# An attention and mixture-of-experts kernel: first loads interleaved, first scores placed behind four rounded half blocks

## The chip, the cores and the metric

The kernel runs on one core of a Trainium2 chip. The metric is the time of one execution in device microseconds (us). The core has five engines with a queue each: TensorE (PE, with its weight loads PEld), VectorE (DVE), ScalarE (ACT), GpSimd (POOL) and SyncE (SP), which only issues DMA transfers. An engine works through its own queue in the order in which the program was written out for it; semaphores order the engines among each other.

## What is computed

```python
def reference(**kwargs):
    attn_out = _attn_ref(**attn_kwargs)              # 4 batches, 8 heads, 576 positions, head size 64
    x = attn_out.transpose(0, 2, 1, 3).reshape(B * S, H * D)     # 2304 tokens x 512
    x = _moe_ref(x=x, **moe_kwargs)                  # (sigmoid(x @ w_gate) * (x @ w_val)) @ w_out
    return _moe2_ref(x=x, **moe2_kwargs)             # 8 experts, two per token, relu, 512 -> 1024 -> 512
...
def _attn_ref(q, k, v, phi):
    a = softmax(phi, axis=2)                         # over the positions, 32 memory slots per head
    k_m = np.einsum('bhsm,bhsd->bhmd', a, k)
    v_m = np.einsum('bhsm,bhsd->bhmd', a, v)
    attn = softmax(q @ k_m.T / sqrt(64))             # 32 scores per position and head
    return attn @ v_m
```

(The softmax lines are shortened here.) Everything is float32 at the interface.

## The kernel before, in words

**Stages.** The program opens with attention for batch 0 and with the preparation of the three weight matrices of the first network, runs the first network batch by batch while the attention of the next batch goes along, routes the tokens, and ends with the eight experts. The change touches the opening alone, about the first 50 us, but it moves instructions up to about 150 us. From there on all five queues hold the same instructions in the same order in both kernels.

**Preparing the weights.** The 18 blocks of `wg`, `wv` and `wo` (six of each, 128x1024 values of 64 bits) arrive as 36 half blocks through four buffers (`ws2`, `WB = 4`; a tile is named `w64`). `rounded` turns one half block into a rounded float32 half: ACT converts the low words (L335), DVE builds the high words in two instructions (`pw` at L337, then L338), POOL adds the two (L339). Only when POOL is done is the buffer free for the load of the half block four places on, which SP issues (L324). When both halves are there, ACT squares the block for its scale (L369; L365 for `wo`), and `norm2` (L92 to L101) makes a power-of-two scale out of the sum: a small matmul `pmx` and a few short DVE instructions, the first of which (L97) waits for that matmul.

**Attention of batch 0.** `features` exponentiates `phi` (DVE L216, ACT L218, DVE L219 and L220). `memory` turns it over on PE (L178, L181), copies it out on ACT (L179, L182), sums keys and values over the positions (PE L191, 40 instructions for each of two groups of heads, ACT L193), and puts the result into `kbd` and `vb` (PE L199, ACT L203 and L205). `values_scale` squares `vb` (ACT L228) and gives the scale `sv0` through `norm2`. `attention` then computes the scores in three pieces (PE L269 and L266; DVE L273, L277, L281 to L283; ACT L278; POOL L284), and turns them over into `x` (PE L292, ACT L299, DVE L300).

**First network.** For each of six units `u`, `fold` multiplies the values into the weights of gate and value (DVE L237, POOL L240, PE L247, ACT L249, DVE L250: called a fold below), and `stage1` runs three pieces of 24 matmuls each (L430) with ACT and DVE behind each (L433 to L437). Batch 1 follows with six more folds. The six blocks of `wo` are split in two halves of float16 by ACT and DVE (L382, L383), and `stage2` (L448) uses them.

**What sets the order.** The code hands out work in turns: a turn of `weights` is about one half block, a turn of `attentions` one step of the attention. A scheduler then orders each engine's queue by priority, where `ahead_by` moves the attention forward; `behind(d, o)` forces an instruction `d` behind an instruction `o`. Before the change, the first three turns go to the attention (its loads are already out by then), five to the weights, and then one of each in turn until `sv0` is known. The first maximum over the scores (L273) is forced behind the latest `pw`/L338 pair that was written out before it (`self.shifted`).

Of the kernel before, what the change touches and what calls it, by code (L numbers as in the profile page):

```python
# [67 lines left out]
class Kern:  # L68
# [16 lines left out]
    def norm2(self, pool, m, tag, before=1, n=1, floor=0):  # L85


        nc = self.nc
        for _ in range(before):
            yield  # L90
        pt = self.pr.tile([P, 512], F32, tag="pr", name="pmx")[:, :n]
        d = nc.tensor.matmul(pt, self.onef, m, start=True, stop=True)  # L92
        if self.mark is not None:
            self.behind(d, self.mark)

        h, s, iv = (pool.tile([P, n], I32, tag=tag + c, name=tag + c) for c in "hsi")
        nc.vector.tensor_scalar(h, pt.bitcast(I32), 24, 23, op0=ALU.logical_shift_right, op1=ALU.logical_shift_left)  # L97
        if floor:
            nc.vector.tensor_scalar(h, h, floor << 23, None, op0=ALU.max)
        nc.vector.tensor_scalar(s, h, -1, 204 << 23, op0=ALU.mult, op1=ALU.add)  # L100
        nc.vector.tensor_scalar(iv, h, 50 << 23, None, op0=ALU.add)  # L101
        return s.bitcast(F32), iv.bitcast(F32)

    def consts(self):
# [5 lines left out]
        self.idf = cp.tile([P, P], F32, name="idf")  # L110
        nc.vector.tensor_scalar(self.idf, jp, 0.0, None, op0=ALU.is_equal)
        self.onef = cp.tile([P, P], F32, name="onef")
# [48 lines left out]
    def att_first_loads(self, b):  # L161
        for x in (("phi", 0), ("phi", 1), ("kv0", 0), ("kv1", 0)):
            self.att_load(b, *x)
        self.wload_next()
        for x in (("kv0", 1), ("kv1", 1), ("q", 0), ("q", 1)):
            self.att_load(b, *x)
        for _ in range(WB - 1):
            self.wload_next()

# [40 lines left out]
    def features(self, b):  # L210

        nc, a2, al = self.nc, self.a2, self.al
        for g in range(2):
            t = al[(b, "phi", g)]
            mx = a2.tile([P, 1], F32, tag="pmx", name="pmx")
            nc.vector.tensor_reduce(mx, t, axis=AX.X, op=ALU.max, negate=True)  # L216
            sm = a2.tile([P, 1], F32, tag="psm", name="psm")
            nc.scalar.activation(t, t, AF.Exp, bias=mx, accum_out=sm)  # L218
            nc.vector.tensor_scalar(sm, sm, 1e-9, None, op0=ALU.add)  # L219
            nc.vector.reciprocal(sm, sm)  # L220
            self.rsum[(b, g)] = sm
            yield
# [30 lines left out]
    def attention(self, b):  # L253
# [4 lines left out]
        def scores(u):  # L258
# [17 lines left out]
            ex = (a2 if u < 2 else self.a1).tile([P, n, M], F32, tag="ex" if u < 2 else "ex2", name="ex")  # L276
            nc.vector.tensor_tensor(ex, sc, mx.unsqueeze(2).to_broadcast([P, n, M]), op=ALU.subtract)  # L277
            nc.scalar.activation(ex, ex, AF.Exp, scale=0.125)  # L278
# [52 lines left out]
    def rounded(self, t, v):  # L331
# [4 lines left out]
        w = self.px.tile([P, DM], F32, tag="px", name="pw").bitcast(I32)  # L336
        nc.vector.tensor_scalar(w, hi, 3, 0x3FFFFFFF, op0=ALU.logical_shift_left, op1=ALU.bitwise_and)  # L337
        self.shifted = nc.vector.scalar_tensor_tensor(v, hi, -0x40000000, w, op0=ALU.bitwise_and, op1=ALU.bitwise_or)  # L338
# [571 lines left out]
    def build(self):  # L910
# [26 lines left out]
        self.whalves = [(k, u, h) for k, u in self.wjobs for h in range(2)]  # L937
        self.wts, self.mark, self.wanted = [], None, []
        self.att_first_loads(0)
# [48 lines left out]
        turns(atts, atts, atts)  # L988
        turns(*[weights] * FIRST)
        while not self.tokens_ready:  # L990
            turns(*[weights] * (4 if self.sv else 1), atts)
# [154 lines left out]
```

## Time and profile before

| | |
|---|---|
| median of three timed runs | 881.49 us (880.47 to 883.07) |
| the profiled execution | 876.4 us |
| its span, from first to last instruction | 873.9 us |
| PE busy / DVE / ACT / POOL, whole span | 798.6 / 465.5 / 443.9 / 225.4 us |
| mean granted TensorE clock | 0.962 |

The span is cut into 40 equal slices of about 21.8 us on the profile's page; a digit there is the busy share in tenths. A row of the timeline reads: start in us, length in us, engine, line of the code, operation, what it writes and reads, how many; in brackets, how long the engine stood idle before it, and what ended that. SPq is SP's queue issuing a transfer. The lines are those of the code before.

### The profile page before, as it was taken

To read this page: it belongs to the slowest core of one execution; us is meant where nothing else is said; L and a number is where in the kernel's file an instruction comes from. 1 tells how busy PE (TensorE), PEld (TensorE's weight loads), DVE (VectorE), ACT (ScalarE), POOL (GpSimd) and SP (SyncE) were. 2 spreads that over 40 slices of the span, in tenths; PEclk is the share of its full clock that TensorE was granted. 3 is DMA by queue.
4 is the path that set the end of the run, shared out by engine and by line. 5 is a ranking of instruction groups with operands and counts; after the bars stand their busy time and mean duration, and the time that the engine had idled before them with its cause. 6 is when DMAs were issued, how large, how long until landed. Compare 5 with 4: busy or idle time off the path is not lost.

```text
span 873.9 us, 16775 instructions
## 1 busy us (share of the span) xinstructions
PE 798.6 (91%) x6531; PEld 524.7 (60%) x6531; DVE 465.5 (53%) x1269; ACT 443.9 (51%) x859; POOL 225.4 (26%) x237
## 2 busy tenths in 40 slices
PE   5157889999999988999999999999999999999995
PEld 4145767657667755766566555665747566574752
DVE  3788798545638687873453146644635435350210
ACT  4658757415554565672243356644736545461320
POOL 1565441001202130204114442102223132222112
PEclk9559889999999999999999999999999999999998
DMA  9778658432121566547692989536766757452113
GB/s 309 258 247 293 222 148 281 137 73 79 26 80 26 176 212 218 170 169 186 200 319 61 177 166 266 144 110 143 193 159 99 174 139 201 78 127 37 23 17 43
DMA packets 125841, 135.15 MB, mean 155 GB/s; under 512 B 71744, under 2 KB 88256, under 8 KB 125248
## 3 DMA queue, kind: packets, MB, share of 16 engines
q1 hardware_dynamic: 115712, 113.30, 44.2%
q0 software_dynamic: 10048, 20.76, 13.1%
q8 instruction: 52, 0.85, 0.4%
q14 instruction: 29, 0.24, 0.1%
HBM read 87.97 MB, written 30.86 MB: 136 GB/s over the span
## 4 chain that ended last, share of the span: by engine, by line
PE 72%; DVE 10%; DMA 9%; ACT 5%; issue 2%; POOL 1%; SPq 1%; POOLq 0%; DVEq 0%; ACTq 0%
PE py L791 23%; PE ph L777 21%; PE px L448 12%; PE pg L430 11%; DMA f<-w 2%; PE pv L247 2%; PE pa L269 1%; DVE hl L383 1%; DVE pw L337 1%; ACT hl L382 1%; DVE w L338 1%; DMA st<-kv 1%; DVE pg L435 1%; DMA xt<-row 1%; DMA w<-wo 1%
## 5 line engine op out<-in xcount | busy, mean ns | idle before, releaser
L430 PE MATMUL pg<-x,wq 128*128 128x192 f16 x1728 | 167.1, 254 | 16.0 <-ACT wq L249 7.2
L430 PEld LDWEIGHTS <-wq 128*128 128x128 f16 x1728 | 149.8, 101 | 34.8 <-issue 11.4
L791 PEld LDWEIGHTS <-hT 128*128 128x128 f16 (+1 forms) x960 | 99.8, 105 | 104.7 <-DVE hT L783 0.8
L448 PE MATMUL px<-wo,gT 128*128 128x512 f16 x648 | 148.8, 380 | 1.9 <-DVE ones L490 1.5
L797 POOL DMA_INDIRECT out<-y,mts x40 | 64.6, 1615 | 208.2 <-ACT y L796 206.1
L791 PE MATMUL py<-w2a,hT 128*128 128x512 f16 (+1 forms) x480 | 105.2, 379 | 0.3 <-DVE hT L783 0.3
L791 PE MATMUL py<-w2b,hT 128*128 128x512 f16 (+1 forms) x480 | 104.9, 379 | 0.0
L448 PEld LDWEIGHTS <-gT 128*128 128x128 f16 x648 | 62.0, 98 | 69.9 <-issue 5.2
L777 PE MATMUL ph<-xe,w1a 128*128 128x312 f16 (+2 forms) x768 | 103.3, 296 | 0.0
L777 PE MATMUL ph<-xe,w1b 128*128 128x312 f16 (+2 forms) x768 | 103.0, 296 | 0.0
L783 DVE TENSOR_TENSOR hT<-r,hT 128x312 f16<-128x312 f32 (+2 forms) x128 | 57.4, 480 | 83.8 <-ACT hT L782 83.3
L796 ACT ACTIVATE y<-py,css 128x512 f32<-128x512 f32 (+1 forms) x40 | 27.5, 686 | 131.3 <-PE py L791 126.8
L777 PEld LDWEIGHTS <-w1b 128*128 128x128 f16 x768 | 75.2, 98 | 27.1
L777 PEld LDWEIGHTS <-w1a 128*128 128x128 f16 x768 | 75.0, 98 | 27.1
L781 ACT ACTIVATE r<-ph 128x312 f32<-128x312 f32 (+2 forms) x128 | 49.7, 428 | 74.1 <-PE ph L777 69.1
L598 POOL DMA_INDIRECT meta<-mt,vi x36 | 37.2, 1033 | 123.7 <-DVE vi L595 98.5
L762 POOL DMA_INDIRECT xg<-xs,mts x40 | 43.9, 1098 | 86.0 <-DMA xe<-xg 53.0
L433 ACT ACTIVATE sg<-pg,gs 128x384 f32<-128x384 f32 x72 | 41.7, 579 | 43.0 <-PE pg L430 42.7
L435 DVE SCALAR_TENSOR_TENSOR pg<-sg,pg 128x384 f32<-128x384 f32 x72 | 40.2, 558 | 35.9 <-PE pg L430 22.7
L794 DVE TENSOR_TENSOR css<-mts,iw 128x1 f32<-128x1 f32 (+1 forms) x40 | 6.4, 163 | 94.5 <-ACT y L796 90.3
L782 ACT CAST hT<-r 128x312 f16<-128x312 f32 (+2 forms) x128 | 53.2, 458 | 0.9
L436 ACT ACTIVATE gT<-pg 128x384 f16<-128x384 f32 x72 | 34.9, 484 | 33.6 <-DVE pg L435 31.6
(314 smaller groups left out, 947.0 us busy)
## 6 DMA issues: line engine op xcount, KB each, us to landing
wo<-w SPq DMA_DIRECT2D x48, 512.0 KB, 5.1
st<-kv SPq DMA_DIRECT2D x16, 512.0 KB, 5.8
f<-w SPq DMA_DIRECT2D x16, 512.0 KB, 5.5
wsp<-hl SPq DMA_DIRECT2D x16, 512.0 KB, 3.5
w<-wg SPq DMA_DIRECT2D x12, 512.0 KB, 5.0
w<-wv SPq DMA_DIRECT2D x12, 512.0 KB, 4.8
w<-wo SPq DMA_DIRECT2D x12, 512.0 KB, 4.8
out<-z SPq DMA_DIRECT2D x23, 256.0 KB, 3.0
```

The source lines that it names most:

```text
L430: nc.tensor.matmul(p[:, f, :], w[:, l, g, j, f * P : (f + 1) * P], x[:, r, g, ch * QC : (ch + 1) * QC], start=n == 0, stop=n == 5)
L433: nc.scalar.activation(sg, ps[0], AF.Tanh, scale=self.gate_scale(b, u))
L435: nc.vector.scalar_tensor_tensor(pv, sg, 1.0, pv, op0=ALU.add, op1=ALU.mult)
L448: nc.tensor.matmul(p, g[:, l, f % 2, t * P : (t + 1) * P], self.wob[f // 2][:, r, f % 2, :], start=f + i == 0, stop=f == FT - 1 and i == 2)
L598: d = nc.gpsimd.indirect_dma_start(out=self.meta, out_offset=bass.IndirectOffsetOnAxis(ap=vi[:, t, k : k + 1], axis=0), in_=mt[:, t, k, :] ...
L762: self.nc.gpsimd.indirect_dma_start(out=xg.rearrange("p a b -> p (a b)"), out_offset=None, in_=self.xs[:rows, :], in_offset=bass.IndirectO ...
L777: nc.tensor.matmul(p[:, : t1 - t0], w1[:, l, k, f * P : (f + 1) * P], xe[:, x, t0:t1], start=n == 0, stop=n == 3 * KT - 1)
L781: nc.scalar.activation(r, p[:, : t1 - t0], AF.Relu, scale=2.0 ** -19)
L782: nc.scalar.copy(self.hT[:, 0, f, t0:t1], r)
L783: nc.vector.tensor_sub(self.hT[:, 1, f, t0:t1], r, self.hT[:, 0, f, t0:t1])
L791: nc.tensor.matmul(py, self.hT[:, l, f, i * P : i * P + m], w2[:, w, f, :], start=n == 0, stop=n == 3 * F2T - 1)
L797: d = nc.gpsimd.indirect_dma_start(out=self.out, out_offset=bass.IndirectOffsetOnAxis(ap=mt[:m, 0:1], axis=0), in_=y[:m], in_offset=None, ...
```

## The change

The first loads come in another order: in place of all keys, values and queries around one half block of weights, with the other three half blocks at the end, the half blocks now stand between the keys and the queries. After the five turns of the weights, turns go to the attention alone until the first scores are written out, so that four half blocks (and no more) stand ahead of them; the roundings that are written out later, and the first DVE instruction of every later `norm2`, are forced behind the first subtraction of the scores (`self.less`). The first instruction on `phi` is forced behind the making of the unit matrix `idf` (`self.made`).

```diff
         h, s, iv = (pool.tile([P, n], I32, tag=tag + c, name=tag + c) for c in "hsi")
-        nc.vector.tensor_scalar(h, pt.bitcast(I32), 24, 23, op0=ALU.logical_shift_right, op1=ALU.logical_shift_left)
+        d = nc.vector.tensor_scalar(h, pt.bitcast(I32), 24, 23, op0=ALU.logical_shift_right, op1=ALU.logical_shift_left)
+        if self.less is not None:
+            self.behind(d, self.less)
...
-        nc.vector.tensor_scalar(self.idf, jp, 0.0, None, op0=ALU.is_equal)
+        self.made = nc.vector.tensor_scalar(self.idf, jp, 0.0, None, op0=ALU.is_equal)
...
     def att_first_loads(self, b):
-        for x in (("phi", 0), ("phi", 1), ("kv0", 0), ("kv1", 0)):
-            self.att_load(b, *x)
-        self.wload_next()
-        for x in (("kv0", 1), ("kv1", 1), ("q", 0), ("q", 1)):
-            self.att_load(b, *x)
-        for _ in range(WB - 1):
-            self.wload_next()
+        for x in (("phi", 0), ("phi", 1), ("kv0", 0), ("kv1", 0), "w", ("kv0", 1), ("kv1", 1), "w", "w", ("q", 0), "w", ("q", 1)):
+            if x == "w":
+                self.wload_next()
+            else:
+                self.att_load(b, *x)
...
-            nc.vector.tensor_reduce(mx, t, axis=AX.X, op=ALU.max, negate=True)
+            d = nc.vector.tensor_reduce(mx, t, axis=AX.X, op=ALU.max, negate=True)
+            if b == 0:
+                self.behind(d, self.made)
...
-            nc.vector.tensor_tensor(ex, sc, mx.unsqueeze(2).to_broadcast([P, n, M]), op=ALU.subtract)
+            d = nc.vector.tensor_tensor(ex, sc, mx.unsqueeze(2).to_broadcast([P, n, M]), op=ALU.subtract)
+            if self.less is None:
+                self.less = d
...
-        nc.vector.tensor_scalar(w, hi, 3, 0x3FFFFFFF, op0=ALU.logical_shift_left, op1=ALU.bitwise_and)
+        d = nc.vector.tensor_scalar(w, hi, 3, 0x3FFFFFFF, op0=ALU.logical_shift_left, op1=ALU.bitwise_and)
+        if self.less is not None:
+            self.behind(d, self.less)
...
         turns(atts, atts, atts)
         turns(*[weights] * FIRST)
+        while self.less is None:
+            turns(atts)
```

What follows from it in the queues is shown at three places. A tile's number in the names tells tiles of one name apart; line numbers after L216 differ by 2 to 6 between the two kernels.

ACT's queue at the opening, before: `w64_151` is the first half block, `a_185` and `a_263` the turned-over `phi` of the first and second group of heads.

```order
L179 COPY a_185<-pa_186 128x512
L182 COPY a_185<-pa_192 64x128
L335 ACTIVATE w64_151<-w64_151 128x512
L193 ACTIVATE km_248<-pa_227,psm_175 128x256
L203 COPY kbd_136<-pa_257 64x2x32 x2
L205 COPY vb0_81<-pa_257 64x128
L179 COPY a_263<-pa_264 128x512
L182 COPY a_263<-pa_270 64x128
L193 ACTIVATE km_294<-pa_273,psm_181 128x256
```

The same place on ACT in the change, where `w64_159` and `w64_161` are the second and third half block.

```order
L339 ACTIVATE w64_151<-w64_151 128x512
L179 COPY a_185<-pa_186 128x512
L182 COPY a_185<-pa_192 64x128
L193 ACTIVATE km_247<-pa_226,psm_175 128x256
L339 ACTIVATE w64_159<-w64_159 128x512
L203 COPY kbd_136<-pa_249 64x2x32 x2
L179 COPY a_255<-pa_256 128x512
L205 COPY vb0_81<-pa_249 64x128
L182 COPY a_255<-pa_262 64x128
L339 ACTIVATE w64_161<-w64_161 128x512
L375 ACTIVATE wo0_71,wum_210<-w0_95 128x1024
L193 ACTIVATE km_286<-pa_265,psm_181 128x256
```

Three low-word conversions and a square now stand among the steps of `memory`; the first of them stands ahead of the copy that the sums of the first group wait for.

DVE's queue up to the first maximum of the scores (`smx`), before; `sv0h` is the first instruction of the values' scale and `w0h` that of the first weight scale.

```order
L338 SCALAR_TENSOR_TENSOR w1_96<-w64_171,pw_220 128x512
L337 TENSOR_SCALAR pw_251<-w64_201 128x512
L338 SCALAR_TENSOR_TENSOR w2_97<-w64_201,pw_251 128x512
L337 TENSOR_SCALAR pw_311<-w64_208 128x512
L97 TENSOR_SCALAR sv0h_324<-pmx_322 128x1
L97 TENSOR_SCALAR w0h_298<-pmx_296 128x2
L99 TENSOR_SCALAR sv0h_324<-sv0h_324 128x1
L338 SCALAR_TENSOR_TENSOR w2_97<-w64_208,pw_311 128x512
L100 TENSOR_SCALAR sv0s_325<-sv0h_324 128x1
L101 TENSOR_SCALAR sv0i_326<-sv0h_324 128x1
L273 TENSOR_REDUCE smx_340<-pa_331 128x16
```

DVE at the same place in the change; `w64_167` is the fourth half block, `w64_201` the fifth.

```order
L341 TENSOR_SCALAR pw_213<-w64_161 128x512
L344 SCALAR_TENSOR_TENSOR w1_96<-w64_161,pw_213 128x512
L97 TENSOR_SCALAR sv0h_299<-pmx_297 128x1
L341 TENSOR_SCALAR pw_220<-w64_167 128x512
L101 TENSOR_SCALAR sv0h_299<-sv0h_299 128x1
L344 SCALAR_TENSOR_TENSOR w1_96<-w64_167,pw_220 128x512
L102 TENSOR_SCALAR sv0s_300<-sv0h_299 128x1
L103 TENSOR_SCALAR sv0i_301<-sv0h_299 128x1
L275 TENSOR_REDUCE smx_315<-pa_306 128x16
L279 TENSOR_TENSOR ex_317<-pa_306,smx_315 128x512
L97 TENSOR_SCALAR w0h_354<-pmx_352 128x2
L341 TENSOR_SCALAR pw_327<-w64_201 128x512
```

Six half blocks stood ahead of the first maximum, now four do; the values' scale, which waits for PE, now stands ahead of the fourth half block, and the first weight scale ahead of the fifth.

DVE between the fifth and the sixth fold of batch 0, before: the second subtraction of the fifth fold (`wq_1326`), and the last two half blocks (`wo6`) behind it.

```order
L250 TENSOR_TENSOR wq_1326<-pv_1328,wq_1326 128x512
L338 SCALAR_TENSOR_TENSOR wo6_77<-w64_1236,pw_1385 128x512
L337 TENSOR_SCALAR pw_1390<-w64_1243 128x512
L237 TENSOR_SCALAR ws_1501<-w5s_1027,sv0s_325 128x2
L338 SCALAR_TENSOR_TENSOR wo6_77<-w64_1243,pw_1390 128x512
L435 SCALAR_TENSOR_TENSOR pg_1351<-sg_1376,pg_1351 128x384
```

DVE in the same stretch in the change; `ws_1473` is the scale of the sixth fold, whose subtractions come later still.

```order
L344 SCALAR_TENSOR_TENSOR wo5_76<-w64_1272,pw_1405 128x512
L441 SCALAR_TENSOR_TENSOR pg_1418<-sg_1443,pg_1418 128x384
L341 TENSOR_SCALAR pw_1449<-w64_1355 128x512
L443 SCALAR_TENSOR_TENSOR gT_1416<-pg_1418,gT_1416 128x2x192
L344 SCALAR_TENSOR_TENSOR wo5_76<-w64_1355,pw_1449 128x512
L341 TENSOR_SCALAR pw_1455<-w64_1363 128x512
L239 TENSOR_SCALAR ws_1473<-w5s_1129,sv0s_300 128x2
L344 SCALAR_TENSOR_TENSOR wo6_77<-w64_1363,pw_1455 128x512
L400 TENSOR_SCALAR gs05_1528<-w5i_1130,sv0i_301 128x1
L341 TENSOR_SCALAR pw_1535<-w64_1401 128x512
```

Between the fifth and the sixth fold's subtractions stood two half blocks, and now there are seven. Counted along DVE's queue, 16 half blocks are rounded ahead of the first fold's subtraction before and 13 in the change; 21 and 17 ahead of the second, 26 and 22, 31 and 27, 34 and 29 ahead of the third to fifth, and all 36 ahead of the sixth in both. Of the six splits of `wo`, five stood ahead of the seventh fold's subtraction, and now two do.

## Rows read from the trace of the kernel before

**Rows 1.** The profile's page: span, PE's total, and PE in 40 slices.

```profile
span 873.9 us, 16775 instructions
...
PE 798.6 (91%) x6531; PEld 524.7 (60%) x6531; DVE 465.5 (53%) x1269; ACT 443.9 (51%) x859; POOL 225.4 (26%) x237
...
PE   5157889999999988999999999999999999999995
```

**Rows 2.** Busy time by stage: stretch, length, each engine's busy us, granted clock, DMA.

```profile
20.00:58.00 38.00, 8.78 (x71) 6.21 (x71) 31.66 (x74) 21.51 (x40) 22.00 (x20) 0.54 0.80 262
58.00:111.00 53.00, 43.76 (x523) 37.05 (x524) 43.04 (x92) 42.02 (x88) 25.38 (x22) 0.88 0.72 241
111.00:140.00 29.00, 25.10 (x282) 18.77 (x280) 25.62 (x71) 18.94 (x36) 10.19 (x31) 0.88 0.72 229
140.00:155.00 15.00, 14.43 (x252) 11.12 (x253) 12.68 (x25) 10.35 (x20) 2.71 (x3) 1.00 0.56 184
```

**Rows 3.** The chain of waits in the first 20 us: start, us, what.

```profile
4.58 8.24 DMA st<-kv
...
12.83 6.34 DMA w<-wg
```

**Rows 4.** Timeline of the first 20 us: loads issued, and who waits for them.

```profile
8.20 3.14 SPq L139 DMA_DIRECT2D gT<-q  x4
8.49 0.58 ACT L179 COPY a<-pa 128x512 f32<-128x512 f32 x1 [1.78 <-PE pa L178]
...
9.12 2.87 PE L191 MATMUL pa<-st,a 128*32 128x128 f32 x40 [0.46 <-ACT a L179]
...
11.02 0.71 ACT L335 ACTIVATE w<-w 128x512 int32<-128x512 uint32 x1 [1.79 <-DMA w<-wg]
...
12.58 1.30 POOL L339 TENSOR_TENSOR w<-w,w 128x512 int32<-128x512 int32 x1 [10.95 <-ACT km L193]
...
14.81 1.98 PE L191 MATMUL pa<-st,a 128*32 128x128 f32 x40 [0.47 <-ACT a L179]
...
17.47 0.44 PE L199 MATMUL pa<-idf,km 128*128 128x128 f32 x2 [0.67 <-ACT km L193]
...
17.74 2.79 PE L269 MATMUL pa<-kbd,gT 128*128 128x64 f32 x24
...
19.20 0.69 DVE L337 TENSOR_SCALAR pw<-w 128x512 int32<-128x512 int32 x1 [6.76 <-DMA w<-wg]
```

**Rows 5.** Timeline from the first square to the first matmul of the first network.

```profile
25.22 1.06 ACT L369 ACTIVATE wo<-w 128x1024 bf16<-128x1024 f32 x1 [0.84 <-POOL w L339]
25.76 0.69 DVE L337 TENSOR_SCALAR pw<-w 128x512 int32<-128x512 int32 x1 [1.13 <-DMA w<-wg]
...
27.47 0.16 DVE L97 TENSOR_SCALAR sv0h<-pmx 128x1 int32<-128x1 int32 x1 [1.02 <-PE pmx L92]
...
28.45 0.68 DVE L273 TENSOR_REDUCE smx<-pa 128x16 f32<-128x512 f32 x1
...
53.22 1.26 DVE L237 TENSOR_SCALAR ws<-w0s,sv0s 128x2 f32<-128x2 f32 x1
...
57.91 7.01 PE L430 MATMUL pg<-x,wq 128*128 128x192 f16 x48 [0.72 <-ACT wq L249]
```

**Rows 6.** DVE's groups by line up to 140 us: count, busy us, mean ns.

```profile
L337 DVE TENSOR_SCALAR pw<-w 128x512 int32<-128x512 int32 x36 | 24.1, 686 | 12.6 <-DMA w<-wg 11.6 <-DMA w<-wv 0.6 <-DMA w<-wo 0.5
L338 DVE SCALAR_TENSOR_TENSOR w<-w,pw 128x512 int32<-128x512 int32 x24 | 16.2, 680 | 0.2
...
L383 DVE SCALAR_TENSOR_TENSOR wo<-wo,wos,wo 128x1024 f16<-128x1024 f32 x5 | 6.5, 1290 | 0.6 <-ACT wo L382 0.6
```

**Rows 7.** Timeline of DVE: the sixth fold's subtractions.

```profile
128.22 1.28 DVE L250 TENSOR_TENSOR wq<-pv,wq 128x512 f16<-128x512 f32 x2
```

**Rows 8.** Timeline of PE: the same four transposes of `phi`, early and later.

```profile
7.36 1.09 PE L178 MATMUL pa<-idf,phi 128*128 128x128 f32 x4 [7.36 <-DVE new L866]
...
65.99 0.60 PE L178 MATMUL pa<-idf,phi 128*128 128x128 f32 x4
```

More of the change, by code (lines that the diff above doesn't have):

```diff
@@ L937, in build @@
         self.whalves = [(k, u, h) for k, u in self.wjobs for h in range(2)]
-        self.wts, self.mark, self.wanted = [], None, []
+        self.wts, self.mark, self.less, self.wanted = [], None, None, []
         self.att_first_loads(0)
```

## The prediction

> **What bounds the kernel now.** The page comes first: PE is busy for 798.6 of 873.9 us, and its slices stand at 8 or 9 from the fourth slice to the last but one [rows 1]. Only the first three slices, some 65 us, are far from full, so a change to the opening is worth what it moves the moment from which PE is full. Busy time by stage [rows 2] says when that is. From 20 to 58 us PE works 8.8 of 38 us and DVE 31.7, from 58 to 111 us PE 43.8 and DVE 43.0 of 53, from 111 to 140 us PE 25.1 and DVE 25.6 of 29, and from 140 to 155 us PE 14.4 of 15. Up to 140 us, then, neither engine is full for long; DVE, which rounds half blocks and finishes both the folds and the pieces of the first network, is the busier one while PE waits. From 140 us PE is full. The first matmul of the first network starts at 57.9 us [rows 5].
>
> The timeline then shows why 57.9. DVE rounds the first half block when it lands at 11.0 us, and stands idle for 6.8 us until the second lands at 19.2 [rows 4]. That transfer was issued at 12.83 and took 6.3 us [rows 3], since four transfers of queries stood ahead of it from 8.2 us on [rows 4]. The first maximum of the scores comes at 28.45 us and the scale of the first fold at 53.2 [rows 5].
>
> **The change, part by part.** I follow the second half block, the first scores, the first fold, and then what is left to do behind it.
>
> *The loads.* The second half block is now issued where the first query was, at 8.20 us. Its landing isn't known. The two prices in the same stretch are 6.3 us (half block) and 8.2 us (keys, issued at 4.58 into the same crowd) [rows 3]; I take the longer, as its neighbours are as many, and get 16.4 instead of 19.2: **2.8 us sooner**, 4.7 at most, 0 at least (first rival). The first half block stays where it was, so it lands at 11.0. The queries come one to two transfers later; they are wanted only by the scores, which I place at 21.5 us below, so they stay hidden up to there.
>
> *ACT's new order.* The first low-word conversion now stands ahead of the copy that the first sums wait for. The copy was done at 9.1 us; now it waits for the landing at 11.0, 0.7 us of conversion and 0.6 us of its own, to 12.3: the sums start 3.2 us later than 9.12 [rows 4]. The next conversion stands ahead of the second group's copies and waits for 16.4. So: conversion to 17.1, `kbd` and copy to 18.1, sums of 2.0 us to 20.1; on ACT meanwhile the third conversion, the square of the first block (1.06 us and its readout) and then `km` to 21.0; two transposes to 21.5; 16 of the 24 score instructions at 2.79/24 us each, 1.9 us, to 23.4 [rows 4, 5]. The small matmul for the values' scale stands right behind, so DVE's `sv0h` can start at about 23.9. It stands ahead of the fourth half block. DVE, whose second and third half block cost 1.34 us each (24.1/36 + 16.2/24) [rows 6], is done at 19.1 and waits **4.8 us**. Fourth half block and first maximum follow: 25.4 instead of 28.45. Behind the first subtraction DVE waits again, for the first weight scale: POOL 1.3 us, a square of 1.25 us with its readout and a small matmul, against nothing to do: **1.7 us**. Two waits of before go away, 1.1 us for a half block and 1.0 us for the same small matmul [rows 5]. Net, waits cost 6.5 - 2.1 = **4.4 us**.
>
> *Fewer half blocks ahead of the fold.* By the queue's order 15 half blocks are rounded ahead of the first fold's scale now, and 10 in the change: 5 x 1.34 = **6.7 us** sooner.
>
> *First fold.* 2.8 + 6.7 - 4.4 = **5.1 us** sooner: scale at 48.1, first network's matmul at about 52.8.
>
> *What is given back.* The half blocks haven't gone. From the first fold's subtraction to the sixth's, DVE now rounds 23 of them and not 20: 3 x 1.34 = 4.0 us on the engine that is 81% to 88% busy there [rows 2]. Against it, three of the six splits of `wo` (1.3 us each, 3.9 us) move behind the seventh fold. There PE is full, so a split costs nothing as long as DVE has room; it has 15 - 12.7 = 2.3 us of it [rows 2], so 1.6 us of the 3.9 don't fit. The give-back lies between 1.7 us (the splits make up for the half blocks, and only the overflow counts) and 4.0 us (the splits were never in the way) where nothing else goes wrong. I take 2.5, nearer to the low end, since DVE has idle time in both stretches.
>
> *Parts at nothing.* `idf` ahead of `phi` lets the first transposes start when the exponential is done instead of at 7.36, but their copy now waits for 11.0 anyway; that hides the gain of it. The order constraints on later roundings and scales have their price in the waits above.
>
> **Sum.** 5.1 - 2.5 = 2.6 us. The profiled execution took 876.4 us (span 873.9 and 2.5 around it); it becomes 873.8. The median of the runs shown lies 5.1 us above the profiled execution, at 881.5; it becomes **878.9**. A measurement of this kernel tells about 0.3%, 2.6 us, from no change, so the forecast lies just on that bound.
>
> [...]
>
> **Rivals.** *The loads gain nothing* (0.10). Transfers in flight share the engines, so the second half block may land at about 19.2 in spite of its place. For it: the keys issued at 4.58 took 8.2 us with everything behind them. Against it: 19.2 - 8.2 would be 11 us, longer than either row [rows 3, 4]. The 2.8 us are gone: 881.7.
>
> *The scores run at half clock* (0.10). [...]
>
> *The half blocks catch up: slower* (0.12). Between the fifth and sixth fold DVE now has seven half blocks, not two: 5 x 1.34 = 6.7 us more in one place, on an engine that has 3.4 us of room in that stretch [rows 2]. The last of them is followed by POOL's 1.3 us and a square, on which a DVE instruction ahead of the sixth fold's subtraction waits; some 2 us of it uncovered. If no room is found, 8.7 us stand against 5.1: 3.6 us slower, 885.1. It decides when the sixth fold's subtraction comes later than 128.2 us [rows 7].
>
> *Nothing is given back* (0.20). If PE was held up by waits in turn rather than by DVE's load, as 19% idle DVE time from 58 to 111 us allows [rows 2], the whole 5.1 us stay, or up to 7.0 if the half block lands after 6.3 us: 876.4 to 874.5.
>
> **How the numbers follow.** The forecast (2.6 us, by its own terms 1.1 to 4.4) has 0.48, half of it beyond 0.3%. With *nothing given back* faster has 0.44; the two rivals at no change and the other half of the forecast give same 0.44; slower has 0.12. The range runs from 874.5, the end of the last rival, to 884.0, short of the slower one's 885.1; it leaves out about one in ten above and less below.
>
> **What would show it.** Right: the second half block rounded at 15 to 17 us; the copy behind the first conversion at about 11.7; DVE idle for 4 to 5 us ahead of `sv0h`; first maximum near 25.4; first matmul of the first network near 52.8; the sixth fold's subtraction before 128; from 155 us on everything shifted by the same amount. Wrong: a second half block at 19; score instructions at twice 0.116 us; the first matmul later than 56; a wait of several us on the last half block ahead of the sixth fold; or a late start of PE's full stretch in spite of an early first fold.

## The result: 0.8% slower

The changed kernel takes 888.52 us (median of 6 runs, 887.98 to 893.15), the kernel before beside it 881.45 us (6 runs, 879.75 to 883.07). The ratio is 1.0085, with a 95% interval from 1.0064 to 1.0105. A second comparison, among the experiments below, gave 1.0080 [1.0057, 1.0104]. The change is slower by some 7 us. The forecast was 878.9 us, and slower had a chance of 0.12.

The page of the changed kernel answers to [rows 1]. PE has the same 6531 matmuls in a longer span; its second and third slices are higher than before, its sixth (some 110 to 132 us) is at 4 and not at 8.

```profile
span 886.5 us, 16763 instructions
...
PE 807.9 (91%) x6531; PEld 530.8 (60%) x6531; DVE 467.5 (53%) x1269; ACT 443.9 (50%) x859; POOL 227.4 (26%) x237
...
PE   4467848999999999899898999999999999999995
```

Busy time by stage, with the stretches of [rows 2], one more ahead and one behind: stretch, length, busy us of PE, PEld, DVE, ACT and POOL, granted clock, DMA share, GB/s.

```profile
0.00:20.00 20.00, 8.12 (x92) 5.34 (x92) 6.62 (x19) 8.28 (x18) 4.87 (x12) 1.00 0.95 306
20.00:58.00 38.00, 19.30 (x116) 15.72 (x117) 26.30 (x66) 19.68 (x41) 17.85 (x17) 1.00 0.69 221
58.00:111.00 53.00, 42.97 (x538) 35.67 (x537) 42.82 (x95) 39.54 (x83) 23.40 (x21) 0.94 0.79 257
111.00:140.00 29.00, 17.04 (x161) 14.41 (x161) 21.92 (x51) 15.60 (x32) 13.34 (x33) 0.71 0.55 159
140.00:155.00 15.00, 13.44 (x211) 9.06 (x209) 13.99 (x33) 12.03 (x19) 3.54 (x3) 1.00 0.97 341
155.00:170.00 15.00, 14.53 (x229) 11.17 (x216) 10.41 (x19) 8.90 (x19) 0.61 (x1) 1.00 0.20 59
```

Between 20 and 58 us PE is busy for 10.5 us more than before (against a second profile of the kernel before, in which PE ran the scores more slowly, it is 6.7 us: 19.3 and 12.6); between 111 and 140 us it does 17.0 us where it did 25.1 before. So something was won at the start and lost there. The timeline of PE and DVE in the opening shows the first half, beside [rows 4] and [rows 5]:

```profile
10.45 0.69 DVE L341 TENSOR_SCALAR pw<-w 128x512 int32<-128x512 int32 x1 [5.00 <-DMA w<-wg]
...
15.82 0.70 DVE L341 TENSOR_SCALAR pw<-w 128x512 int32<-128x512 int32 x1 [3.45 <-DMA w<-wg]
...
17.47 2.52 PE L191 MATMUL pa<-st,a 128*32 128x128 f32 x40 [0.96 <-ACT a L179]
...
21.14 3.52 PE L271 MATMUL pa<-kbd,gT 128*128 128x64 f32 x16
...
25.01 0.16 DVE L97 TENSOR_SCALAR sv0h<-pmx 128x1 int32<-128x1 int32 x1 [6.42 <-PE pmx L92]
...
30.27 0.16 DVE L97 TENSOR_SCALAR w0h<-pmx 128x2 int32<-128x2 int32 x1 [2.32 <-PE pmx L92]
...
48.26 0.79 DVE L239 TENSOR_SCALAR ws<-w0s,sv0s 128x2 f32<-128x2 f32 x1
...
52.62 0.82 PE L436 MATMUL pg<-x,wq 128*128 128x192 f16 x4 [0.87 <-ACT wq L251]
```

The second half block is rounded at 15.82 us instead of 19.20, DVE then waits twice, for the values' scale and for the first weight scale, and the first fold's scale comes at 48.26 instead of 53.22. These points in time are the prediction's to within 1.2 us; the two waits, 6.42 and 2.32 us, are longer than forecast. A score instruction takes 0.22 us here (3.52/16) and 0.116 in [rows 4] (2.79/24); four transposes take 1.09 and 0.60 us in [rows 8]. The lower level of TensorE, or half clock, stands below for the longer of these durations, its upper level for the shorter, and neither for more. The second half shows around the sixth fold, where [rows 7] had the subtractions at 128.22:

```profile
125.03 0.92 DVE L239 TENSOR_SCALAR ws<-w5s,sv0s 128x2 f32<-128x2 f32 x1
...
126.79 1.96 PE L249 MATMUL pv<-w,vs 64*32 64x256 f32 x32 [5.19 <-POOL vs L242]
...
130.07 1.15 ACT L371 ACTIVATE wo<-wo,w5i 128x1024 bf16<-128x1024 f32 x1 [2.87 <-POOL wo L345]
...
131.37 0.78 ACT L220 ACTIVATE phi<-phi,pmx 128x576 f32<-128x576 f32 x1
...
132.14 1.05 ACT L251 CAST wq<-pv 128x512 f16<-128x512 f32 x2
132.76 0.82 PE L436 MATMUL pg<-x,wq 128*128 128x192 f16 x4 [4.01 <-ACT wq L251]
...
133.64 1.27 DVE L252 TENSOR_TENSOR wq<-pv,wq 128x512 f16<-128x512 f32 x2
```

PE waits 5.19 us for the sixth fold's scaled values, because DVE computes the scale `ws` only behind the half blocks that it catches up with. Then PE waits 4.01 us for the fold's cast, because ACT has a square of the last block ahead of it, which waits 2.87 us for POOL, and behind that an exponential. So the lead of 5 us at the first fold is a lag of 5.4 us at the sixth fold's subtraction.

### The profile page after: what moved, and what is told of

The parts are those of the page before. It is cut to its first block, busy times and chain, and to the rows that moved or that the text cites. A ratio compares the mean times of both kernels' runs of the same rounds, so it can differ in the third digit from the quotient of the medians.

```text
span 886.5 us, 16763 instructions
## 1 busy us (share of the span) xinstructions
PE 807.9 (91%) x6531; PEld 530.8 (60%) x6531; DVE 467.5 (53%) x1269; ACT 443.9 (50%) x859; POOL 227.4 (26%) x237
## 3 DMA queue, kind: packets, MB, share of 16 engines
q1 hardware_dynamic: 115712, 113.30, 44.4%
## 4 chain that ended last, share of the span: by engine, by line
PE 72%; DMA 9%; DVE 9%; ACT 5%; issue 3%; POOL 1%; SPq 1%; DVEq 0%; POOLq 0%; ACTq 0%
PE py L797 22%; PE ph L783 20%; PE px L454 12%; PE pg L436 11%; PE pa L271 2%; DMA f<-w 2%; DMA w<-wg 2%; PE pv L249 1%; DVE hl L389 1%; DMA wo<-w 1%; PE pa L191 1%; DMA st<-kv 1%; DVE pw L341 1%; DMA xt<-row 1%; ACT hl L388 1%
## 5 line engine op out<-in xcount | busy, mean ns | idle before, releaser
L604 POOL DMA_INDIRECT meta<-mt,vi x36 | 36.3, 1009 | 124.7 <-DVE vi L601 100.8
L768 POOL DMA_INDIRECT xg<-xs,mts x40 | 45.7, 1142 | 85.8 <-DMA xe<-xg 49.9
L439 ACT ACTIVATE sg<-pg,gs 128x384 f32<-128x384 f32 x72 | 41.7, 579 | 47.3 <-PE pg L436 44.4
```

Of the source, the lines that this page charges most:

```text
L439: nc.scalar.activation(sg, ps[0], AF.Tanh, scale=self.gate_scale(b, u))
L604: d = nc.gpsimd.indirect_dma_start(out=self.meta, out_offset=bass.IndirectOffsetOnAxis(ap=vi[:, t, k : k + 1], axis=0), in_=mt[:, t, k, :] ...
L768: self.nc.gpsimd.indirect_dma_start(out=xg.rearrange("p a b -> p (a b)"), out_offset=None, in_=self.xs[:rows, :], in_offset=bass.IndirectO ...
```

## The experiments

All are compared with the kernel before on the same chip. One table first. "Twelfth fold" is the start of its subtraction on DVE, and the next column is DVE's busy and idle time up to there. The last column is when DVE reaches one common instruction, the last reciprocal (`ssm`) of the second batch's scores; behind it every engine has the same order in the kernel before and in the change. It comes from one profile each, and is out of step with the timed ratio by up to 4 us (idf_late: 6.5 us late, 2.7 us slower; no_stall_again: 1.6 us late, 2.1 us faster), so it says where time is lost better than how much.

| kernel | ratio [95%] | twelfth fold, us | DVE busy + idle, us | common instruction, us |
|---|---|---|---|---|
| before_again | 1.0007 [0.9990, 1.0023] | 155.1 | 117.6 + 37.5 | 195.7 |
| change_again | 1.0080 [1.0057, 1.0104] | 165.3 | 118.7 + 46.6 | 205.3 |
| loads_alone | 1.0018 [1.0003, 1.0033] | 156.2 | 115.0 + 41.2 | 196.2 |
| loop_alone | 1.0032 [1.0012, 1.0051] | 158.4 | 118.1 + 40.3 | 198.4 |
| idf_late (loads and loop) | 1.0031 [1.0009, 1.0053] | 162.1 | 118.8 + 43.3 | 202.1 |
| old_loads (idf and loop) | 1.0090 [1.0063, 1.0116] | 166.1 | 118.2 + 47.9 | 206.1 |
| nine_turns | 1.0051 [1.0026, 1.0076] | 161.0 | 116.6 + 44.4 | 201.7 |
| nine_first | 1.0036 [1.0018, 1.0053] | 157.5 | 117.0 + 40.5 | 199.0 |
| double_round | 1.0086 [1.0054, 1.0118] | 165.7 | 124.7 + 41.0 | 205.4 |
| double_convert | 1.0007 [0.9993, 1.0021] | 157.0 | 117.5 + 39.5 | 197.2 |
| double_late | 1.0044 [1.0028, 1.0061] | 157.0 | 119.1 + 37.9 | 197.5 |
| loads_no_stall | 0.9976 [0.9962, 0.9990] | 155.9 | 116.6 + 39.3 | 196.5 |
| no_stall_again | 0.9976 [0.9960, 0.9993] | 156.7 | 117.2 + 39.5 | 197.3 |
| warm | 1.0145 [1.0119, 1.0172] | 162.8 | 118.2 + 44.6 | 202.8 |
| warm_short | 1.0175 [1.0141, 1.0209] | 163.0 | 118.2 + 44.9 | 203.6 |
| no_stall_warm | 1.0071 [1.0042, 1.0100] | 156.3 | 116.9 + 39.4 | 197.6 |

**Where the loss lies: before_again and change_again.** Both kernels unchanged, profiled a second time on one chip. "DVE's account" in the expectations is this idea: up to the twelfth fold DVE has a fixed amount of work, so that point moves only by DVE's idle time or by more work.

> The kernel before, unchanged, profiled a second time. If the stretch behind 195 us belongs to the execution and the chip: the common instruction at 195.4 us comes within 1 us of the first profile, and the rest takes anything from 678 to 686 us; ratio 1.000 within 0.002. If it belonged to the program: the rest takes 678.5 us again.

> The change, unchanged, profiled a second time beside the kernel before. DVE's account: the common instruction 7.5 to 9 us later than in the kernel before (203 to 204.5 us), the rest of the execution within 2 us of that of the kernel before on this chip, 7 to 9 us slower in all. If half of the loss arose behind 195 us: the rest 4 us longer than that of the kernel before.

Busy time of the kernel before, cut at the subtractions of the first, fifth and twelfth fold, and from the common instruction to the end; below it the same for the change.

```profile
0.00:58.10 58.10, 23.13 (x183) 17.66 (x183) 36.46 (x89) 29.52 (x61) 24.11 (x30) 1.00 0.86 281
58.10:115.30 57.20, 48.47 (x554) 40.87 (x558) 45.63 (x101) 43.53 (x91) 26.87 (x23) 0.88 0.69 228
115.30:155.10 39.80, 35.90 (x506) 27.76 (x499) 35.51 (x89) 27.87 (x53) 11.61 (x33) 0.96 0.70 227
...
195.70:873.00 677.30, 655.93 (x4969) 419.80 (x4966) 327.75 (x930) 330.82 (x628) 160.03 (x148) 0.99 0.56 136
```

```profile
0.00:53.60 53.60, 23.41 (x185) 17.60 (x185) 29.47 (x78) 24.94 (x53) 20.09 (x26) 1.00 0.77 247
53.60:111.80 58.20, 48.91 (x559) 41.06 (x556) 45.12 (x103) 41.72 (x86) 25.23 (x23) 0.88 0.78 254
111.80:165.30 53.50, 39.73 (x501) 30.02 (x498) 44.13 (x99) 34.16 (x63) 18.33 (x38) 0.84 0.61 195
...
205.30:882.50 677.20, 656.04 (x4968) 419.80 (x4966) 328.03 (x930) 330.87 (x628) 160.09 (x148) 0.99 0.55 136
```

Behind the common instruction the two executions take 677.3 and 677.2 us (the last stretch is cut 0.1 us short): nothing of the loss is there. In the first pair of profiles it is 678.5 us before and 682.9 in the change, but that profile of the kernel before was of an execution 5.1 us below its timed median. Ahead of the twelfth fold DVE does 279 and 280 operations in 117.6 and 118.7 us. The third number of each row is the point. Up to the first fold DVE does 7.0 us less in the change, and that is all of its lead: its idle time there is 24.1 us, not 21.6. The 7.0 us come back between the fifth and the twelfth fold, as 8.6 us more work, and with them 5.1 us more of idle time (9.4 against 4.3); between them it is 1.5 us more. In all 9.1 us of idle time and 1.1 us of work: the 10.2 us by which the twelfth fold is late. Loads slow down with it, 247 GB/s and not 281 up to the first fold; a buffer is loaded again only when its half block has been rounded.

**Is DVE's account what counts? double_round, double_convert, double_late.** Idle and busy time always add up to the time; that shows nothing yet. So work was added to the kernel before in three places.

```
 def rounded(self, t, v, times=1):              # double_round: times=2 for wo
-        nc.vector.tensor_scalar(w, hi, 3, 0x3FFFFFFF, ...)
+        for _ in range(times):
+            nc.vector.tensor_scalar(w, hi, 3, 0x3FFFFFFF, ...)
...
+        if junk is not None:                   # double_convert: wo alone
+            nc.scalar.activation(junk, lo.bitcast(U32), AF.Copy, scale=2.0 ** -29)
...
-        nc.vector.scalar_tensor_tensor(o[:, 1, :, cols], pv, ...)
+        for _ in range(2 if b == 1 else 1):    # double_late
+            nc.vector.scalar_tensor_tensor(o[:, 1, :, cols], pv, ...)
```

> The kernel before, with DVE's first rounding operation (the shifted low bits, 0.67 us) done twice for each of the twelve half blocks of wo; the result stays the same. Theory of DVE's account (up to the twelfth fold DVE has a fixed amount of work, and what counts is that work plus DVE's idle time): 12 x 0.6 to 0.67 = 7 to 8 us slower than the kernel before, 889 to 891 us. Theory of waits in turn (DVE has idle time in that stretch and swallows more work; what counts is which single wait ends last): 0 to 4 us slower, 882 to 887 us.

> The kernel before, with one more conversion on ACT (0.66 us, into a scratch tile) for each of the twelve half blocks of wo. Theory of DVE's account: ACT has 54 us of idle time up to the twelfth fold, so within 2 us of the kernel before, 881 to 885 us. Theory that ACT, which holds the casts of the folds, is what the folds wait for: 7 to 8 us slower, 889 to 891 us.

> The kernel before, with the last DVE operation of a piece of the first network (0.56 us) done twice in the 18 pieces of the second batch, all of them behind 190 us: 18 x 0.56 = 10 us more of DVE's work, the result unchanged. DVE's account up to the twelfth fold alone: TensorE is full there and DVE has room, so 0 to 3 us slower. If DVE's work binds everywhere: 8 to 10 us slower.

Against a median of 877.49 us before, 7.2 to 8 us more on DVE ahead of the twelfth fold cost 7.5 us (0.0086 x 877.5; 4.7 to 10.4 by the interval). The same on ACT cost 0.6 us, not to be told from nothing. So DVE's account held between the first fold and the twelfth, where the added work stood; the theory of waits in turn, which lets DVE swallow more work, did not. Work added in the opening, ahead of the first fold, and work added on POOL were not tried.

Double_late was not quite what its expectation says. In its trace four of the 18 repeated operations, 2.2 us, run at 145 to 157 us, ahead of the twelfth fold, which comes 1.9 us later than in before_again; two run at 159 to 165 us, and twelve behind 197 us. The whole cost 3.9 us. If the four are paid in full, the 7.8 us behind the twelfth fold cost 1.7; that split is not shown by itself.

DVE's busy time in the first two, up to their twelfth folds (third number; ACT's is the fourth):

```profile
0.00:165.70 165.70, 110.81 (x1241) 87.30 (x1241) 124.67 (x287) 101.01 (x202) 62.27 (x85) 0.77 0.72 232
```

```profile
0.00:157.00 157.00, 108.13 (x1237) 86.55 (x1238) 117.47 (x275) 108.12 (x214) 63.17 (x85) 0.78 0.76 245
```

**The change part by part: loads_alone, loop_alone, idf_late, old_loads.** The new order of the loads alone; the loop alone; the change without idf's constraint; the change with the old loads. The two other constraints of the change, on later roundings and scales, need no kernel: with and without them every engine's instructions stand in the same order.

```
+        for x in (("phi", 0), ("phi", 1), ("kv0", 0), ("kv1", 0), "w", ...):   # loads_alone: as in the change
...
+        while not self.scored:                 # loop_alone; set behind the first subtraction
+            turns(atts)
...
-            if b == 0:                         # idf_late
-                self.behind(d, self.made)
...
-        for x in (("phi", 0), ("phi", 1), ("kv0", 0), ("kv1", 0), "w", ...):   # old_loads: as before the change
```

> The kernel before with the new order of the first loads alone; nothing else of the change. Half blocks rounded ahead of the subtractions of folds 1 to 6: 14, 20, 24, 30, 33, 36 (before 16, 21, 26, 31, 34, 36; change 13, 17, 22, 27, 29, 36). Catch-up theory (the change loses because too few half blocks are handed out early and seven have to be caught up between the fifth and the sixth fold): only three are left for that stretch, so no loss, and the second half block lands near 15.8 us instead of 19.2: 877 to 882 us, sixth fold's matmuls near 124 us. Load theory (the new order of the loads makes later transfers late, and that is the loss): 885 us or more, with half blocks waiting for landings between 100 and 130 us.

> The kernel before with the loop alone, which hands out the first scores right behind four half blocks' rounding; old loads, idf in its old place. Half blocks ahead of folds 1 to 6: 12, 18, 23, 28, 30, 36. By DVE's account: the early first fold (near 50 us) gives nothing, since DVE only does later what it didn't do before; idle time is added by the stall for the scores and by the catch-up: 3 to 7 us slower than the kernel before, sixth fold's matmuls at 126 us or later. If the early scores are worth what they seem: 2 to 5 us faster.

> The change without the one constraint that puts idf ahead of the features' maxima. ACT then has the first copies ahead of the first conversion, as in the kernel before. Half blocks ahead of folds 1 to 6: 13, 17, 22, 27, 29, 36, as in the change. If idf's place costs (through ACT's order: the copy behind a landing, TensorE waiting and at its lower level): values' scale at 20 to 23 us and by DVE's account 2 to 4 us of the loss gone, 3.5 to 6 us slower than the kernel before. If the few turns of the weights are all of it: 7 to 9 us slower, as the change.

> The change with the old order of the first loads. Half blocks ahead of folds 1 to 6: 12, 17, 22, 27, 29, 36, so the catch-up between the fifth and the sixth fold is as in the change. Catch-up theory: as slow as the change, 886 to 891 us (second half block again near 19 us, first fold one to three us later than the change's 49.8), sixth fold's matmuls at 127 us or later. Load theory: back at the kernel before, 880 to 883 us.

The loop alone is the clearest. Its first fold starts at 47.0 us, 8 us ahead of the kernel before (the first matmul on `vs`), its opening has hardly more idle time (22.1 us up to the first fold), and still it is 2.8 us slower (0.0032 x 882.1): the early fold is worth nothing, and the catch-up costs (8.3 us idle between the fifth and the twelfth fold, 4.3 in before_again). The load theory falls: with the old loads the change is no better, 1.0090. The loads alone lose 1.6 us instead of winning 2; the likely reason is that DVE waits 5.42 us at 27.61 for the first weight scale with four half blocks ahead of it, and filling that wait (loads_no_stall, below) gained. Idf's place is dear: loop and loads without it 1.0031, with it 1.0080 to 1.0085; loop without it 1.0032, with it 1.0090. By the timed runs that is 4 to 5 us. Between idf_late and the change at least two differences of order stand ahead of the first maximum: in the change ACT's first conversion stands ahead of the first copy, and PE has the small matmul of the values' scale behind 16 score instructions (at 24.44 us) and not ahead of them all (at 19.95 us). Which of the two costs was not tried, and old_loads also rounds one half block less than loop_alone ahead of the second to fifth fold. By the one profile of idf_late it is less, 1.6 to 3.2 us at the common instruction; the size is not settled, its sign is.

**More turns of the weights: nine_turns and nine_first.** Nine more behind the first unit, or four more (FIRST = 9) ahead of the first scores.

```
-                turns(weights, weights, weights)              # nine_turns
+                turns(*[weights] * (6 if u < 1 else 3))
```

> The change with nine more turns of the weights behind the first unit's three pieces (six a piece, not three). The opening is the change's; half blocks ahead of folds 1 to 6: 13, 18, 23, 29, 35, 36, and five splits of wo ahead of the seventh fold as before the change (two in the change). Catch-up theory: the first fold stays near 49.8 us and the sixth is no later than 124 us, so the lead of the opening is kept in part: 875 to 880 us, faster than both. Opening theory (the half clock scores and the waits of the opening disturb what follows): no better than the change, 886 to 890 us. Load theory: also 886 to 890 us.

> The change with nine turns of the weights ahead of the first scores, not five: half blocks ahead of folds 1 to 6 are 16, 21, 26, 31, 34, 36, the counts of the kernel before, with the new loads and the new order constraints kept. Catch-up theory: no pile ahead of the sixth fold, but no early first fold either: 879 to 883 us, sixth fold's matmuls near 123 to 125 us. Load theory or opening theory (the constraints themselves cost): 885 us or more.

In nine_turns all half blocks but one are rounded ahead of the fifth fold, and the splits stand where they stood in the kernel before. It is 3 us better than the change and 4.5 us slower than the kernel before: the sixth fold's matmuls start at 129.9 us, later than in the change (126.8). The lead of the first fold is gone by the third (81.4 against 82.0 us), since the half blocks that weren't done in the opening are now done there. So the pile ahead of the sixth fold is part of the loss, and taking it away does not bring the lead back. Nine_first has the half blocks of the kernel before and is slower by 3.2 us, near the 3 us by which DVE's idle time is longer.

**The stall filled: loads_no_stall, twice.** The loads alone, with the two scales' first operation behind the rounding that has been handed out.

```
-        nc.vector.tensor_scalar(h, pt.bitcast(I32), 24, 23, ...)
+        d = nc.vector.tensor_scalar(h, pt.bitcast(I32), 24, 23, ...)
+        if tag in ("sv0", "w0"):
+            self.behind(d, self.shifted)
```

> The kernel before with the new order of the loads, and with DVE's first operation on the values' scale and on the first weight scale put behind the half blocks handed out so far, so that five and six half blocks stand ahead of them (four and four in the loads alone, three and four in the change). Half blocks ahead of folds 1 to 6: 16, 21, 26, 31, 34, 36, as in the kernel before. Theory of DVE's account: the two to three us that the second half block comes sooner are kept, because the 5.4 us stall of the loads alone is filled with work: 879 to 881.5 us, 1 to 3 us faster than before. Rival (what comes sooner from memory is given back as later landings): no better than the loads alone, 883 to 886 us.

> The loads without the stall once more, on another chip perhaps. If its gain is real: 1 to 3 us faster than the kernel before again, and its common instruction ahead of that of the kernel before profiled beside it. By the one profile at hand it would come 1 us behind: then within 1.5 us of the kernel before in either direction.

It is the one version that beats both kernels, by 0.24% on two chips, with intervals that end short of 1. That is below the 0.3% set as the bound at the outset. Nor do the profiles show where it comes from: DVE waits 2.58 us, not 5.42, for the first weight scale, but the common instruction comes 0.8 and 1.6 us later than in the second profile of the kernel before, and the profiled execution was slower (span 876.7 against 873.0 on the same chip). I take it as a small gain by the timed runs and leave its place open.

**TensorE's level in the opening: warm, warm_short, no_stall_warm.** Matmuls of ones into a scratch bank while PE waits: 16 + 14 + 4 in the change, 16 + 4 in the change, 16 + 4 in loads_no_stall.

```
+    def warm(self, n):
+        pt = self.pr.tile([P, 512], F32, tag="pr", name="pw0")
+        for _ in range(n):
+            d = self.nc.tensor.matmul(pt[:, :P], self.onef, self.onef, start=True, stop=True)
...
```

> The change, with 34 matmuls of 128 x 128 ones into a scratch bank on TensorE while it waits in the first 20 us (16 ahead of the first transposes, 14 behind them, 4 behind the second transposes); they change no result. Half clock theory (TensorE stands at its lower level when the scores come, because it waited): 16 score instructions take 1.9 instead of 3.5 us, the second sums 2.0 instead of 2.5, the values' scale comes 2 to 3 us sooner and DVE stalls 2 to 3 us less: 886 to 888 us against some 890 for the change on this chip. If the stall is ACT's new order alone: as the change, 889 to 891 us.

> The change with 20 matmuls of ones into a scratch bank (16 ahead of the first transposes, 4 behind them); unlike the run with 34, ACT's and DVE's order stay those of the change. Half clock theory: first sums 1.4 to 1.5 us instead of 2.5, 16 score instructions 1.9 instead of 3.5, the values' scale at 22 to 23.5 us instead of 25.0. Theory of DVE's account: what DVE stalls less at the values' scale (1.5 to 3 us) is what the whole gains, so 4.5 to 7 us slower than the kernel before, against 7 to 8.5 for the change. If idle time in the opening does not carry through: 7 to 9 us slower.

> The kernel of the loads without the stall, with the same 20 matmuls of ones in the opening. By DVE's account the 2.6 us that DVE still waits for the first weight scale there go in part when TensorE's opening runs at its upper level: 3 to 5 us faster than the kernel before (the loads without the stall: 2.1 us faster). If the level is not what that wait hangs on: 2 us faster, as without the matmuls.

PE in the opening of the run with 34 matmuls, and of the one with 20:

```profile
6.13 0.60 PE L186 MATMUL pa<-idf,phi 128*128 128x128 f32 x4
...
12.15 1.43 PE L201 MATMUL pa<-st,a 128*32 128x128 f32 x40 [2.18 <-ACT a L187]
...
27.18 3.68 PE L281 MATMUL pa<-kbd,gT 128*128 128x64 f32 x32
```

```profile
6.33 0.60 PE L186 MATMUL pa<-idf,phi 128*128 128x128 f32 x4
...
11.98 2.52 PE L201 MATMUL pa<-st,a 128*32 128x128 f32 x40 [4.04 <-ACT a L187]
...
21.55 3.52 PE L281 MATMUL pa<-kbd,gT 128*128 128x64 f32 x16
```

Both rates are there. In the longer run the first sums took 1.43 us instead of 2.52, and a score instruction 0.115 us (3.68/32) instead of 0.22 (3.52/16). So the scores of the change run at the lower level. That PE's waits in the change are the reason is not shown: in the second profile of the kernel before, where no wait of PE between 9 us and the scores is longer than 0.67 us, a score instruction took 0.22 us as well (5.22/24), and not the 0.116 of [rows 4]. So it did in loads_no_stall (5.35/24), again with no wait longer than 0.67 us.

```profile
18.03 5.22 PE L269 MATMUL pa<-kbd,gT 128*128 128x64 f32 x24
```

The level in the opening thus differs between executions of one kernel (0.116 and 0.22 us for a score instruction), and the kernel before loses nothing by it that its common instruction would show (195.4 us with the fast scores, 195.7 with the slow ones). What the upper level would have saved in the change was not measured: with 34 matmuls ACT's order changed as well, and `km` came 6 us later; with 20 the order stayed and PE, after it had waited 4.04 us for ACT's copy, was at the lower level again (2.52 us for the first sums). So the first run missed its 886 to 888 us and the second its 4.5 to 7: all three were 5 to 8 us slower than the same kernel without the matmuls (by the ratios, against 1.0085 and 0.9976). In their profiles all three lose it behind the common instruction; the last section comes back to that.

## Why the prediction was wrong

**The loads: right.** 16.4 us was forecast for the second half block, 15.82 was measured. The 306 GB/s that the change moved over the first 20 us were no ceiling: from 14 to 24 us it moved 384 GB/s, and from 79 to 84 us the kernel before moved 420 (last number of each row, the change first).

```profile
14.00:24.00 10.00, 7.77 (x67) 6.23 (x64) 2.70 (x4) 6.09 (x17) 2.60 (x2) 1.00 1.05 384
```

```profile
79.00:84.00 5.00, 3.90 (x61) 2.88 (x60) 3.61 (x13) 4.42 (x12) 1.10 (x2) 1.00 1.04 420
```

**ACT's new order: right, and dearer.** The copy ran at 11.03 us, behind the first conversion; the values' scale came at 25.01, not 23.9, and the waits were 6.42 and 2.32 us, not 4.8 and 1.7. Of the missing 2.2 us, 0.5 is DVE being ready for the values' scale at 18.6 us and not at 19.1. The rest goes with slow matmuls, the subject of the half clock rival: 3.52 us for 16 score instructions and 2.52 us for the second sums, 2.1 us more than the sum had. I gave it 0.10 as an alternative; it was a part of what happened. What makes them slow is not shown. PE standing still in the change does not explain it alone, since the kernel before has the same slow scores in its second profile, with PE at work from 9 us on; and the granted clock is recorded as 1.00 from 20 to 58 us in the change. With matmuls ahead of them the four transposes took 0.60 us, without 1.11. The first fold came on time in part by luck: up to its scale DVE's idle time grew by 2.0 us (23.58 against 21.56) where 1.6 was forecast, so most of what the two waits cost too much was made up elsewhere.

**Fewer half blocks ahead of the fold: the step that failed.** "5 x 1.34 = 6.7 us sooner" went into the sum as a gain, and under "What is given back" I took back 2.5. The first fold did come at 48.26 us (forecast 48.1), but that was no gain at all: DVE had done 7.0 us less, and did it later. The rows that told me DVE was the busier engine up to 140 us [rows 2] held the answer. In this stretch, work of DVE that was moved behind a milestone made the milestone earlier and nothing else: loop_alone has its first fold 8 us sooner and is 2.8 us slower. By the prediction's own terms the account would have been 2.8 sooner, 4.4 for waits, and 6.7 in and out again: 1.6 us slower before anything else, a slower kernel. (Two slips of reading changed nothing: PE's fourth slice in [rows 1] is a 7, and the 4.4 us at the upper end of the gain follow from no terms given; 5.1 - 1.7 is 3.4.)

**What is given back: mis-sized even so.** 1.7 to 4.0 us was the range; from the first fold's subtraction to the twelfth's the change lost 14.7 us (4.5 ahead to 10.2 behind, second profiles). 8.1 of them are DVE's work that came back, 6.6 are idle time, 5.1 of it behind the fifth fold. Costing the catch-up by DVE's load alone missed those: a scale, a square and a cast stand in line behind half blocks on three engines in turn.

**The slower rival: came true by its own test.** It was to decide when the sixth fold's subtraction came later than 128.2 us; it came at 133.64. The time that I gave it, 885.1, is 3.4 us below the measured one, and the pile is not all of the loss: without it (nine_turns) 4.5 us stayed.

**The rest.** "Idf at nothing" was wrong in that its place brought ACT's new order with it. "From 155 us on everything shifted by the same amount" held over the last 677 us of the second pair of profiles; in the first pair the last stretch differs by 4.4 us.

## What to carry to other kernels

Before crediting a milestone that comes earlier, ask whether the engine that sets the pace has done less by then: compare its busy time up to the point from which something else is the bound, and count only its idle time. Which engine that is can be tested with added work: 7.2 to 8 us more on DVE cost 7.5, on ACT nothing that could be told. And when a small operation that waits for another engine is put ahead of ready work on a queue that runs in order, look for its wait first; here one of 0.16 us held DVE for 6.42.

## What the runs showed of the hardware

From the common instruction to the end every kernel but double_late has the same instructions in the same order. Leaving out the three with matmuls of ones, profiled executions took 677.3 to 679.4 us there in three kernels on one chip, 678.1 to 678.6 in three on a second, 685.5 to 686.8 in four on a third, and 680.8 and 682.0 in two on a fourth. One execution each from two chips can therefore differ by up to 9 us in this stretch alone, more than the loss that was to be explained. The time of the common instruction is steadier: 195.4 and 195.7 us in two profiles of the kernel before, 203.7 and 205.3 in two of the change.

The record of the granted clock does not show the slow matmuls in the opening of the change. It gives 1.00 from 20 to 58 us, while four transposes there took 1.12 us, near the 1.09 of [rows 8] and not the 0.60. The same holds for the second profile of the kernel before: 1.00 from 0 to 58.1 us, with scores of 0.22 us in it.

```profile
34.87 1.12 PE L296 MATMUL pa<-idf,ex 128*128 128x128 f32 x4 [4.65 <-POOL ex L288]
```

Twenty matmuls of ones in the opening made loads_no_stall 8 us slower (1.0071 against 0.9976), though its common instruction comes at 197.6 us against 196.5 and 197.3. It loses the time behind that point (688.6 us to the end; warm_short on the same chip 687.0, the two kernels without such matmuls 680.8 and 682.0; warm 682.6 on a chip where three others took 678.1 to 678.6), part of it in waits of PE for the transposed rows of the router, 3.94 us in the longest:

```profile
424.38 0.49 PE L486 MATMUL pl<-wr,xt 128*128 128x16 f16 x12 [3.94 <-DMA xt<-row]
```

Without the matmuls that wait is 2.62 us. Why kernels with a few matmuls more at the start lose time that late stays open.
